# Rows of x by ACT's queue, key weights by SyncE's, and new instruction orders in a four-layer attention kernel

## The chip, the cores and the metric

The kernel runs on one core of a Trainium2 chip. The time is the device time of one execution in microseconds (us); lower is better. Several executions are timed and the median is given. One further execution is recorded by the profiler; its trace is what the profile lines below come from. TensorE (PE) multiplies matrices, VectorE (DVE) and ScalarE (ACT) do elementwise work, GpSimd (POOL) small constants and masks, and SyncE (SP) issues most of the DMAs. Each engine executes its own list of instructions in order and waits on semaphores for the others.

## The reference

The input x has 2048 rows of 512 numbers. Four layers follow one another, of two kinds, and the two weights sets A and B are each used twice:

```python
x = x + A(layernorm(x), A_wqkv, A_wo)   # linear attention, 32 heads of 16
x = x + B(layernorm(x), B_wqkv, B_wo)   # sliding window of 256, softmax
x = x + A(layernorm(x), A_wqkv, A_wo)
x = x + B(layernorm(x), B_wqkv, B_wo)
```

In A, `phi(t) = where(t > 0, t + 1, exp(t)) + 1e-6` is applied to queries and keys, the sums `kv = sum_s phi(k) v` and `z = sum_s phi(k)` run over all 2048 rows, and the output is `phi(q) kv / (phi(q) z + 1e-6)` times `wo`. In B, each row attends to itself and the 255 rows before it.

## The kernel before, in words

The rows are 16 tiles of 128. The work has three parts with two barriers between them, because the sums of a layer A need all rows. Part one (`layer_a_keys`) loads the tiles, normalises them, and computes the keys of the first layer A (`a_k`), their products with the normalised rows (named g) and the queries (`a_q`). After the first barrier, part two (`middle(2)`) runs for each tile the output of layer A, layer B, and the keys of the second layer A. After the second barrier, part three (`middle(3)`) does the same for the last two layers and writes the result.

A tile's normalisation (`norm`) is: statistics on DVE (line 374), their aggregation (line 375), adding epsilon (line 377 on DVE, 379 on POOL), the power -1/2 on POOL (line 380), and subtract and scale on DVE (line 381). The result is transposed: the first five tiles by TensorE (line 395) with a copy by ACT (line 402), the others by a transposing DMA that SyncE issues (line 389). The key product is line 420, the products g line 524, the queries line 480. `phi` is an exponential on ACT (line 444), a minimum on DVE (line 447) and a maximum, either in one DVE instruction (line 451) or with a second ACT instruction (446) and a DVE one (449).

At the first barrier, copies of the sums (named ge, line 407) feed TensorE, a masked product (line 574) and a reciprocal (line 603) follow on DVE, and the weights of the output are merged on TensorE (line 578). In the layers B, ACT computes the exponentials of the scores (lines 720, 755, 788, 835), DVE or POOL the masks (728, 807; 806), and a copy of the keys (bke, line 661 on ACT, 662 on DVE) is spread by DMA.

The loads are issued ahead of everything else: `setup` lists them for SyncE. `xs(a, b)` loads the rows of tiles a to b-1 and names the load after a, so that x0 and x1 are one tile each (128 KB), x2, x4 and x6 two tiles, x8 and x12 four. `w(...)` loads 512 KB of weights: wAq, wAv and wAk are the query, value and key columns of A_wqkv, and wBn is 1 MB of B_wqkv. A load given an earlier load in its last argument is issued only once that one has landed. In `run`, `play` writes each engine's program. Before the planned instructions, DVE clears a tile, TensorE runs nine matmuls on it and then `fill` ones that the plan places (line 277); their results are used by nobody. ACT waits for the cleared tile and issues the two halves of the key weights wAk (line 1117), on which the first two key products wait (`ksem`).

The order of all 2,572 planned instructions, the engine of those that can run on two, and the PSUM bank of each of 1,006 tiles are read from a packed table (`TABLE`, read by `place`); it is the outcome of a search that isn't part of the kernel. `synchronise` then derives the waits from the order. On POOL, an instruction of the names in `LONG` also waits for the last DVE instruction of the names in `SHORT` ahead of it.

## Time and profile before

| | us |
|---|---|
| median of 3 runs | 407.45 |
| lowest and highest | 407.4, 408.07 |
| the profiled execution | 409.25 |
| its span, first to last instruction | 407.4 |
| mean granted TensorE clock | 0.998 |
| busy in the span: TensorE | 386.1 |
| ACT | 350.4 |
| DVE | 349.3 |
| POOL | 125.8 |

A line of a profile view gives start and length in microseconds, then the engine, the line of the kernel, the operation, and the tile it writes, an arrow, and the tiles it reads. `xres` holds the rows of x, `vp` the normalised rows and the keys, `XQ` the transposed rows and the queries, `wA` the weights of layer A, `ps` a bank of PSUM. Square brackets give the idle time ahead of an instruction and what ended it. SPq and ACTq are DMA issues of SyncE and ACT. A busy TensorE is not a TensorE at its peak, since the ends of matmuls are modelled.

### The profile page before, as it was taken

What the parts mean: (1) busy time and instruction counts of PE and PEld (TensorE: products, weight loads), DVE (VectorE), ACT (ScalarE), POOL (GpSimd) and SP (SyncE); (2) the same over time, 40 slices, a digit from 0 to 9 for tenths busy, and PEclk for the clock granted to TensorE, in tenths of its full rate; (3) what the DMA queues carried; (4) which work ended last, traced back from release to release, by engine and by line L of the source; (5) the groups of instructions that cost most, each with busy time, mean ns of one, the idle gap of its engine ahead of it and who ended that gap; (6) DMA issues with size and microseconds to landing.
All of it is one profiled execution on the core that took longest, in us unless ns stands there. A gap on an engine that the chain in (4) does not pass through costs nothing.

```text
span 407.4 us, 17007 instructions
## 1 busy us (share of the span) xinstructions
PE 386.1 (95%) x7394; PEld 255.7 (63%) x7466; DVE 349.3 (86%) x818; ACT 350.4 (86%) x447; POOL 125.8 (31%) x215
## 2 busy tenths in 40 slices
PE   7999999999999999999999999999999989998996
PEld 3644576667475567565656767676656756666674
DVE  5998899999999899888877799998899689777674
ACT  2843559999999999999999368999999999999992
POOL 3588752122243142331602122301203241320130
PEclk9999999999999999999999999999999999999999
DMA  7546324443233425553222100562324433572551
GB/s 253 138 113 163 98 42 107 101 101 81 68 101 78 91 82 121 80 108 80 77 49 56 27 2 2 121 122 69 80 55 101 119 89 68 111 142 77 85 148 40
DMA packets 66986, 37.15 MB, mean 91 GB/s; under 512 B 47648, under 2 KB 62368, under 8 KB 66912
## 3 DMA queue, kind: packets, MB, share of 16 engines
q1 hardware_dynamic: 66080, 34.75, 36.8%
q8 instruction: 59, 0.97, 1.1%
q0 software_dynamic: 288, 0.79, 0.5%
q10 hardware_dynamic: 544, 0.52, 0.4%
q14 instruction: 15, 0.12, 0.1%
HBM read 6.29 MB, written 2.10 MB: 21 GB/s over the span
## 4 chain that ended last, share of the span: by engine, by line
PE 54%; ACT 21%; DVE 14%; issue 5%; DMA 3%; POOL 1%; SPq 1%; POOLq 0%; DVEq 0%
PE ps L420 19%; ACT pb L720 16%; PE ps L856 11%; PE ps L434 8%; PE ps L710 6%; PE ps L480 4%; DVE stats L374 2%; ACT pb L835 2%; PE ps L524 2%; DVE XQ L625 2%; ACT vp L720 2%; DMA xres<-in_A_x_dram 1%; DVE xres L638 1%; DVE vp L451 1%; PE ps L826 1%
## 5 line engine op out<-in xcount | busy, mean ns | idle before, releaser
L720 ACT ACTIVATE pb<-ps 128x1024 bf16<-128x1024 f32 (+2 forms) x216 | 199.4, 1021 | 3.6 <-PE ps L710 2.4
L856 PEld LDWEIGHTS ps<-vB,pb 128*128 128x128 bf16 x2560 | 78.6, 96 | 11.4 <-issue 3.6
L856 PE MATMUL ps<-vB,pb 128*128 128x34 bf16 x2560 | 84.4, 177 | 0.3
L806 POOL TENSOR_SCALAR_AFFINE_SELECT pb<-pb 128x1024 bf16<-128x1024 bf16 x33 | 37.9, 1150 | 106.0 <-DVE pb L807 40.1
L434 PE MATMUL ps<-xT,wBp 128*128 128x128 bf16 x1024 | 69.6, 219 | 0.9 <-ACT pb L720 0.5
L434 PEld LDWEIGHTS ps<-xT,wBp 128*128 128x128 bf16 x1024 | 59.2, 98 | 13.3 <-issue 4.7
L444 ACT ACTIVATE tE<-ps 128x512 bf16<-128x512 f32 x64 | 37.8, 606 | 24.4 <-PE ps L420 9.9
L379 POOL TENSOR_SCALAR ve<-mv 128x1 f32<-128x1 f32 x63 | 16.4, 260 | 130.3 <-DVE mv L375 128.4
L710 PE MATMUL ps<-XQ,kB 32*128 32x256 bf16 (+3 forms) x992 | 48.1, 267 | 3.0 <-DVE o L869 0.5
L420 PE MATMUL ps<-wA,XQ 128*128 128x512 bf16 x175 | 45.3, 379 | 1.7 <-issue 0.5
L638 DVE TENSOR_TENSOR xres<-ps,xres 128x512 bf16<-128x512 f32 x63 | 42.8, 683 | 4.7 <-PE ps L420 4.2
L374 DVE BATCH_NORM_STATS2 stats<-xres 128x6 f32<-128x512 bf16 x64 | 43.2, 681 | 4.0 <-DMA xres<-in_A_x_dram 3.5
L728 DVE TENSOR_TENSOR pb<-pb,tri 128x512 bf16<-128x512 bf16 (+1 forms) x108 | 43.0, 407 | 3.8 <-ACT pb L720 2.9
L380 POOL TENSOR_TENSOR rs<-ve,negh 128x1 f32<-128x1 f32 x64 | 40.3, 630 | 7.6 <-DVE ve L377 2.4
L835 ACT ACTIVATE pb<-ps 128x1024 bf16<-128x1024 f32 x40 | 39.4, 1054 | 1.1 <-PE ps L826 1.1
L480 PE MATMUL ps<-XQ,wA 128*128 128x256 bf16 x256 | 34.1, 273 | 0.4 <-ACT pb L720 0.4
L710 PEld LDWEIGHTS ps<-XQ,kB 32*128 32x128 bf16 x992 | 15.0, 92 | 28.8 <-ACT pb L720 7.6
L420 PE MATMUL ps<-M,XQ 128*128 128x512 bf16 x113 | 30.5, 380 | 2.4 <-issue 0.6
L420 PE MATMUL ps<-wBv,xT 128*128 128x512 bf16 x109 | 30.3, 380 | 2.3 <-issue 1.4
L420 PE MATMUL ps<-wBo,oT 128*128 128x512 bf16 x107 | 28.9, 380 | 2.6 <-DVE tE L447 0.7
L869 DVE TENSOR_TENSOR o<-ps,rc 128x256 bf16<-128x256 f32 x64 | 27.0, 423 | 1.6
L480 PEld LDWEIGHTS ps<-XQ,wA 128*128 128x128 bf16 x256 | 23.6, 98 | 7.5 <-ACT pb L720 0.8
(132 smaller groups left out, 543.8 us busy)
## 6 DMA issues: line engine op xcount, KB each, us to landing
vB<-vS SPq DMA_DIRECT2D x64, 136.0 KB, 2.5
kB<-vp SPq DMA_DIRECT2D x60, 128.0 KB, 2.1
out_dram<-xres SPq DMA_DIRECT2D x9, 128.0 KB, 2.2
wA<-in_A_wqkv_dram SPq DMA_DIRECT2D x2, 512.0 KB, 5.5
xres<-in_A_x_dram SPq DMA_DIRECT2D x2, 512.0 KB, 4.0
pb<-in_B_wqkv_dram SPq DMA_DIRECT2D x1, 1024.0 KB, 6.6
xres<-in_A_x_dram SPq DMA_DIRECT2D x3, 256.0 KB, 5.5
out_dram<-xres POOLq DMA_DIRECT2D x6, 128.0 KB, 2.6
```

Source lines behind the costliest of these rows:

```text
L374: self.on("DVE", "stats", lambda e: e.bn_stats(K.stats[:, t, :], x()), key, dve(512), rd=rd, wr=[("stats", t)], **held)
L380: self.pow = self.on("POOL", "pow", lambda e: e.tensor_tensor(K.rs[:, t, :], K.ve[:, t, :], K.negh[:], ALU.pow), key + 0.03, (640, 690), r ...
L420: m = e.matmul(K.ps(ps), lhs(c), rhs(c), start=c == 0 and not whole, stop=c == 3)
L434: m = e.matmul(K.ps(ps)[:, f * P:(f + 1) * P], w(c, f), xT(c), start=c == 0, stop=c == 3)
L480: m = e.matmul(K.ps(ps)[:, 256 * h:256 * h + 256], K.wA[:, c, f * P:(f + 1) * P], xT(c), start=c == 0, stop=c == 3)
L638: self.on("DVE", "res", lambda e: e.tensor_tensor(K.xres[:, t, :], K.ps(po), K.xres[:, t, :], ALU.add), key, dve(512), rd=[("xres", t)], w ...
L710: m = e.matmul(K.ps(ps[gq])[:, ns * i:ns * i + ns], K.kB[rows, j % 4, 2 * f + b, :, :], K.XQ[rows, f, q:q + ns], start=True, stop=True, ti ...
L720: return e.activation(out(2 * h, 2, ns), i, ACT.Exp, bias=0.0, scale=0.25)
L728: return e.tensor_tensor(x, x, K.tri[:, 0, sh:64].unsqueeze(1).unsqueeze(1).to_broadcast([P, 4, n, 64 - sh]), ALU.mult)
L806: return e.affine_select(out=x, in_=x, compare_op=ALU.is_ge, fill=0.0, base=-2, pattern=[[0, 16], [-2, 64]], channel_multiplier=1)
L835: return e.activation(far(h), i, ACT.Exp, bias=0.0, scale=0.25)
L856: m = e.matmul(K.ps(ps)[:, 34 * u:34 * u + 34], K.P((b // 2) % rp)[:, gq, f, o:o + P], K.vB[:, (b // 2) % 4, b % 2, r, :], start=i == 0, s ...
```

## The change

The loads of tile 1 (x1) and of tiles 2 and 3 (x2) are issued by ACT, ahead of its other work and without a wait. In front of them ACT issues a small read of four pieces of A_wqkv's first columns into an unused row of `kB` (the touch, `tsem`); the first key copy of layer B that SyncE issues (kd) waits for it, because it writes there. The two halves of the key weights become planned loads of SyncE, in its list right behind x0, and every key product waits for its half. The wait of ACT for the cleared tile goes.

All of the table is new. Its entries, decoded, say that SyncE's first issues are x0, wAk0, wAk1, x4, wAq, x6, wAv, x8, a transpose, x12 and wBn; before they were x0, x1, x2, x4, x6, wAq, x12, x8, two transposes and wBn. TensorE's first entries were four fillers, the transpose of tile 0, a filler, the transpose of tile 1, a filler, and the first halves of the keys of tiles 0 and 1; they become two fillers, the transpose of tile 0, four fillers, the transpose of tile 1, and the two halves of tile 0 and then of tile 1. On DVE, tile 1's subtract and scale moves ahead of tile 2's aggregation. On POOL, five constants (c6, c7, c8, c11, c12) move up among the powers of tiles 3 to 8. At the first barrier a copy ge goes from ACT to DVE and a maximum (line 449) from behind it to an earlier place. Further on, 41 instructions change engine: one bke in the first layer B from ACT to DVE, one in the second from DVE to ACT and a copy sc from ACT to DVE, 12 masks of line 806/807 from DVE to POOL and 11 back, five output DMAs from SyncE to POOL and two back, and some copies and memsets. Otherwise neighbours change places, and 364 of the 1,006 tiles have another bank.

```diff
+ACT_LOADS = ("x1", "x2")
...
-        seq += [xs(0, 1), xs(1, 2), w("wAq", "wA", "A_wqkv", 0, 512), xs(2, 4), xs(4, 6), xs(6, 8), xs(8, 12)]
+        def wk(h):
+            return ("wAk%d" % h, lambda e: e.dma_start(K.wA[:, 2 * h:2 * h + 2, 512:1024], K.A_wqkv.rearrange("(k p) c -> p k c", p=P)[:, 2 * h:2 * h + 2, 512:1024]), 262144, [("wAk", h)])
+
+        seq += [xs(0, 1), wk(0), wk(1), xs(1, 2), w("wAq", "wA", "A_wqkv", 0, 512), xs(2, 4), xs(4, 6), xs(6, 8), xs(8, 12)]
...
-            begun.append(self.load(n, f, b, r, key + i if i < 7 else 100.5 + 0.5 * i, begun[i - 4:i - 3] if i >= 6 else []))
+            begun.append(self.load(n, f, b, r, key + i if i < 9 else 100.5 + 0.5 * i, begun[i - 4:i - 3] if i >= 8 else []))
...
-        ps = self.tok("k", t, xT, lambda c: K.wA[:, c, 512:1024], lambda h: [("XQ", t)], key)
+        ps = self.tok("k", t, xT, lambda c: K.wA[:, c, 512:1024], lambda h: [("XQ", t), ("wAk", h)], key)
...
-            ksem, half = [cx.enter_context(nc.semaphore(f"s_key{h}")) for h in range(2)], []
+            tsem, touched = cx.enter_context(nc.semaphore("s_touch")), []
...
                 if name == "ACT":
-                    e.wait_ge(wsem, 1)
-                    for h in range(2):
-                        e.dma_start(self.wA[:, 2 * h:2 * h + 2, 512:1024], self.A_wqkv.rearrange("(k p) c -> p k c", p=P)[:, 2 * h:2 * h + 2, 512:1024]).then_inc(ksem[h], 16)
+
+                    e.dma_start(self.kB[0:1, 3, 0:4, :, :].rearrange("p k n a -> p k (n a)"), self.A_wqkv.rearrange("(k p) c -> p k c", p=P)[0:1, :, 0:128]).then_inc(tsem, 16)
+                    for o in order:
+                        if o.name in ACT_LOADS:
+                            o.emit(e).then_inc(dsem[o.dma[1] % ring], 16)
...
-                    if o.eng != name:
+                    if o.eng != name or o.name in ACT_LOADS:
                         continue
...
-                    if o.name == "k" and len(half) < 2:
-                        e.wait_ge(ksem[len(half)], 16)
-                        half.append(o)
+                    if o.name == "kd" and not touched:
+                        touched.append(1)
+                        e.wait_ge(tsem, 16)
```

## The prediction

> **What bounds the kernel now.** I read the page first, then the windows by stage, then the chain of waits, then the timeline of the first microseconds.

> ```profile
> span 407.4 us, 17007 instructions
> PE 386.1 (95%) x7394; PEld 255.7 (63%) x7466; DVE 349.3 (86%) x818; ACT 350.4 (86%) x447; POOL 125.8 (31%) x215
> ```

> The shares are averages, so the stages decide. In the windows the columns are the stretch, its length, busy time and instructions of PE, weight loads, DVE, ACT and POOL, then the granted clock, the DMA share and GB/s.

> ```profile
> 5.00:10.00 5.00, 4.14 (x24) 1.73 (x23) 3.13 (x9) 1.19 (x2) 1.81 (x6) 1.00 1.02 343
> 10.00:15.00 5.00, 4.95 (x41) 3.47 (x40) 4.93 (x16) 4.22 (x8) 3.56 (x10) 1.00 0.42 123
> ...
> 40.00:45.00 5.00, 4.92 (x64) 2.83 (x67) 3.09 (x6) 2.00 (x4) 4.58 (x8) 1.00 0.77 251
> ...
> 100.00:150.00 50.00, 47.36 (x1013) 30.33 (x1020) 47.43 (x110) 49.15 (x57) 16.03 (x26) 1.00 0.35 86
> 150.00:200.00 50.00, 48.52 (x990) 31.67 (x999) 43.26 (x101) 48.92 (x56) 15.61 (x26) 1.00 0.47 94
> ```

> From 10 us on TensorE has no holes in the first stage (4.95 and 4.92 of 5 us), and DVE is as full as TensorE at 10 to 15. In the attention stage ACT is the full engine (49.15 and 48.92 of 50). So a microsecond saved before 10 us moves the whole first stage, if DVE and TensorE both start sooner; in the attention only ACT's time counts.

> The chain of waits over the start (start, length, engine):

> ```profile
> 1.72 5.19 DMA xres<-in_A_x_dram
> ...
> 6.93 0.71 DVE stats L374
> 7.66 0.18 DVE mv L375
> ...
> 44.50 0.69 DVE kB L407
> 45.19 0.55 DVE XQ L449
> 45.74 0.87 DVE rec L603
> ```

> It begins with a load of rows of x, named x2 in the code (tiles 2 and 3), goes on with DVE, and is on DVE again at the first barrier (44.5 us on: a copy of a sum, a maximum, a reciprocal). The timeline says what the load holds up:

> ```profile
> 6.77 0.40 PE L395 MATMUL ps<-ident,vp 128*128 128x128 bf16 x4
> ...
> 6.93 0.69 DVE L374 BATCH_NORM_STATS2 stats<-xres 128x6 f32<-128x512 bf16 x1 [1.83 <-DMA xres<-in_A_x_dram]
> ...
> 7.76 0.38 DVE L381 TENSOR_SCALAR vp<-xres,mv,rs 128x512 bf16<-128x512 bf16 x1
> ...
> 8.21 0.40 PE L395 MATMUL ps<-ident,vp 128*128 128x128 bf16 x4 [0.81 <-DVE vp L381]
> ...
> 8.44 0.38 PE L277 MATMUL ps<-kB 128*128 128x512 bf16 x1
> ...
> 8.65 1.24 PE L420 MATMUL ps<-wA,XQ 128*128 128x512 bf16 x4
> ...
> 15.95 1.27 DVE L374 BATCH_NORM_STATS2 stats<-xres 128x6 f32<-128x512 bf16 x2
> ```

> DVE executes in order: the statistics of tile 2 wait 1.83 us for x2, and tile 1's normalisation (7.76) stands behind them although tile 1 came long before. TensorE transposes tile 1 at 8.21, runs a filler matmul at 8.44 and starts the first key product at 8.65. Real TensorE work of the stage begins there. At 15.95 come the first statistics of the tiles of x8.

> **The change, part by part.** Decoding the two tables of the diff gives the orders. The same instructions run, apart from the loads.

> *Loads.* SyncE's queue was x0, x1, x2, x4, x6, wAq; it becomes x0, wAk0, wAk1, x4, wAq, x6, wAv, x8. ACT issued the two key-weight halves after waiting for DVE's memset; now it issues a small read of A_wqkv (the touch), x1 and x2 with no wait.

> ```profile
> 0.80 2.37 SPq L294 DMA_DIRECT2D xres<-in_A_x_dram  x5
> ...
> 1.23 0.99 ACTq L1117 DMA_DIRECT2D wA<-in_A_wqkv_dram  x2
> ...
> 7.21 0.60 ACT L402 ACTIVATE XQ<-ps 128x512 bf16<-128x512 bf16 x1 [3.68 <-PE ps L395]
> ```

> The second view below is of the two ACT issues alone, the third a window of one microsecond:

> ```profile
> DMA to landing us min/median/max: 3.9/4.6/5.4
> ...
> 4.00:5.00 1.00, 1.00 (x3) 0.30 (x2) 0.96 (x3) 0.00 (x0) 0.67 (x2) 1.00 0.83 274
> ```

> An issue takes 2.37/5 = 0.47 us on SyncE and 0.50 on ACT. x2 was third on SyncE: issued at 0.80 + 2 x 0.47 = 1.7. As third on ACT, if ACT too begins at 0.8, it is issued at 0.8 + 2 x 0.5 = 1.8. No gain in issue. What lies beside it on the DMA engines is shown by the packets (columns: packets, MB, share) in 0 to 4.25 us, first two lines, and 0 to 5.25 us, last two; q1 is SyncE's queue, q10 ACT's:

> ```profile
> q1 hardware_dynamic: 383, 0.36, 28.5%
> q10 hardware_dynamic: 265, 0.26, 20.2%
> ...
> q1 hardware_dynamic: 500, 0.47, 29.5%
> q10 hardware_dynamic: 427, 0.42, 25.3%
> ```

> In that microsecond q1 gained 0.11 MB and q10 0.16 MB: they share. Before x2 can be complete, x0, x1, wAk0, x2 and most of wAk1 are moved in either order. The best case is that half of wAk1 (0.13 MB) falls behind x2: 0.13 MB / 274 GB/s = 0.48 us sooner. The worst is that ACT's queue starts late, by as much as its whole first issue pair costs on top of the touch, 0.50 + 0.47, less the 0.43 us by which ACT starts earlier (1.23 to 0.80): 0.54 us later. I take 0, the middle. The touch adds an ACT issue of 0.5 us; ACT sat idle for 3.68 us before its first work at 7.21, so it costs nothing, and would cost 0.5 without that idle time. The new wait on the touch stands on SyncE ahead of the first key copy of the sliding layer, with value copies and output DMAs queued behind it; the touch has landed long before. wAq moves up, x6 goes behind it, and x8 behind wAv's 0.5 MB, 1.9 us at that rate. x8 is read only from 15.95 us on, and it no longer follows x12, an equal amount: hidden, and if that cover goes DVE stands up to 1.9 us. x12 and the load of B's weights now come after the first transpose that SyncE issues, with the other transposes behind them; they move up with x8, and I count 0.

> [...]

> *Start of TensorE's work.* The new DVE order puts tile 1's normalisation directly behind tile 2's statistics, ahead of their aggregation: 7.76 - 7.66 = 0.10 us. The new TensorE order has no filler between tile 1's transpose and the key products: 8.65 - 8.44 = 0.21 us. Six fillers instead of five stand ahead of tile 1's transpose (two before tile 0's, four behind it): one more, at most 0.38, which lies in TensorE's 0.81 us of idle there and would cost 0.38 without it. The keys of tile 0 now go as one pair, which needs wAk1 by 8.3 us. It landed at 1.72 + 5.4 = 7.1 as ACT's second issue, and is issued at 0.80 + 2 x 0.47 = 1.7 as SyncE's third: 1.2 us to spare. Term: -0.31 us.

> *First barrier.* The 0.55 us maximum (line 449) leaves the chain ahead of the reciprocal; one copy of a sum (ge) goes from ACT to DVE, ahead of the wait for z, where DVE has room (3.09 of 5 us).

> ```profile
> 47.44 0.84 PE L578 MATMUL ps<-wAo,pqd 128*128 128x512 bf16 x3 [0.35 <-DVE pqd L574]
> ```

> TensorE had other work and stood only 0.35 us here, so at most 0.35 can come back, and at worst the copy (0.69 us on DVE in the chain) comes in its place if it is late: between -0.35 and +0.34. I take -0.30, nearer to the idle time that the row shows.

> *Attention.* One key copy (bke) leaves ACT for DVE:

> ```profile
> L661 ACT ACTIVATE vp<-ps x1: 748/748/748, 156.8 to 156.8; 128x512 bf16<-128x512 f32 x1
> ...
> 154.88 1.89 PE ps L434 x32
> ...
> L806 POOL TENSOR_SCALAR_AFFINE_SELECT pb<-pb x33: 1137/1147/1208, 86.4 to 390.6; 128x1024 bf16<-128x1024 bf16 x33
> ...
> L807 DVE TENSOR_TENSOR pb<-pb,tri x17: 678/682/1103, 87.9 to 381.9; 128x1024 bf16<-128x1024 bf16 x17
> ```

> ACT is full there and DVE has 50 - 43.26 = 6.74 us of room, which says -0.75; but the chain of waits until 156.77 runs on TensorE, which says 0. I take half, -0.37. In the second layer one copy goes from ACT to DVE (sc) and one back (bke): 0. Twelve far masks move from DVE to POOL and eleven back, three output DMAs net from SyncE to POOL, two small memsets change place: nothing on the chain waits for POOL there; without that cover a mask costs DVE 0.68 or POOL 1.15 us. The remaining swaps of neighbours, and other PSUM banks for 364 of 1006 tiles, can close holes or open them; ACT's holes from 100 to 200 us sum to 0.85 + 1.08 = 1.93 us, which bounds both sides. I take 0.

> Sum: -0.10 - 0.21 - 0.30 - 0.37 = -0.98 us. The profiled execution took 409.25 us, of which 407.40 is span; it stands 0.44% above the median of 407.45, and I put the difference on the median: **406.5 us**.

> **The rivals.** *No measurable change, 407.1 us.* The barrier's hole opens elsewhere and bke was hidden; only the 0.31 at the start is kept. For it: DVE is full right after the start (4.93 of 5), so a lead of TensorE may run dry; against it: DVE starts 0.10 sooner too.

> *Slower, 408.5 us.* POOL computes the power that every normalisation waits for. The new order puts five constants among the first nine tiles' powers, which before ran in gaps from 28 us on:

> ```profile
> 32.39 0.21 POOL L328 MEMSET hot<- 128x128 bf16 x1 [0.48 <-DVE tE L447]
> ...
> 32.88 0.36 POOL L337 TENSOR_SCALAR_AFFINE_SELECT hot<-hot 128x128 bf16<-128x128 bf16 x1
> ...
> 28.04 0.12 POOL L328 MEMSET eps<- 128x32 bf16 x1
> ...
> 37.66 0.31 POOL L338 TENSOR_SCALAR_AFFINE_SELECT hot<-hot 128x128 bf16<-128x128 bf16 x1
> ...
> 30.04 0.29 POOL L343 MEMSET eps<- 1x32 bf16 x1
> ...
> L447 DVE TENSOR_SCALAR tE<-tE x64: 229/284/989, 11.9 to 295.3; 128x512 bf16<-128x512 bf16 x64
> ```

> They sum to 1.29 us on a POOL that is 3.56 of 5 busy at 10 to 15, where DVE cannot wait. And DVE's minimum (line 447) has taken up to 0.99 instead of 0.28 us: one such meeting adds 0.7. Together 2.0 us, 406.47 + 2.0 = 408.5. It decides once more than 0.98 + 0.82 = 1.8 us is lost. Against it: POOL has 1.44 us free in that window.
> [...]

> *A larger gain, 405.0 us.* x2 lands 0.48 sooner and half of ACT's 1.93 us of holes close: 406.47 - 0.48 - 0.97. For it: both orders are new throughout; against it: the shared packets.

> **How the numbers follow.** This kernel's runs tell 0.2%, 0.82 us, from no change. Chances: the forecast 0.37, the larger gain 0.13, no change 0.25, slower 0.25. So faster 0.50, same 0.25, slower 0.25. The range goes from the larger gain, 405.0, to a little past the slower rival, 408.7; the forecast's own is 405.9 to 407.0 by the bounds of x2.

> **What would show it.** Right: DVE's wait for x2 still ends near 6.9; the first key product starts near 8.3; TensorE's wait at line 578 is under 0.1; the first stage's last product ends 0.3 sooner; ACT's full stage begins 0.6 sooner. Wrong: normalisations that wait for POOL between 9 and 16 us, a DVE wait for x8 or x6, x2 past 7.4, or new ACT holes between 100 and 200 us.

## The result: slower by 1.3%, and the profile after

The changed kernel takes 413.07 us (median of 4 executions, 411.02 to 413.51) against 407.42 us (407.38 to 408.07) for the kernel before beside it: ratio 1.0125, 95% interval 1.0089 to 1.0161. A second set of executions gave 1.0140 (1.0115 to 1.0166). I had forecast 406.5 us, and a range of 405.0 to 408.7: the sign was wrong and the time lies outside the range. The profiled execution took 413.51 us, 411.8 of it span. In the kernel after, lines stand five further down than before (420 is 425, 374 is 379, 578 is 583).

The head of its page, and the chain of waits over the first 26 us (start, length, what):

```profile
span 411.8 us, 17013 instructions
PE 386.9 (94%) x7395; PEld 255.3 (62%) x7466; DVE 348.6 (85%) x818; ACT 350.9 (85%) x446; POOL 128.5 (31%) x219
```

```profile
0.80 1.21 ACTq L1121
2.44 5.47 DMA xres<-in_A_x_dram
7.93 0.69 DVE stats L379
...
18.29 6.76 DMA XQ<-vp
```

TensorE is as busy as before (386.9 against 386.1 us), so most of the 4.4 us of span are holes. The chain names two of them. It begins no longer with x2 at 1.72 but with the small load (line 1121), whose issue holds ACT's queue for 1.21 us; x2 is on its way from 2.44 and DVE has it at 7.93, before at 6.93. Then a transpose of the first stage takes 6.76 us to land.

The timeline of ACT's queue and of DVE over the same start:

```profile
0.80 1.21 ACTq L1121 DMA_DIRECT2D kB<-in_A_wqkv_dram  x1
2.04 0.85 ACTq L296 DMA_DIRECT2D xres<-in_A_x_dram  x2
```

```profile
2.95 0.69 DVE L379 BATCH_NORM_STATS2 stats<-xres 128x6 f32<-128x512 bf16 x1 [1.75 <-DMA xres<-in_A_x_dram]
...
5.81 0.69 DVE L379 BATCH_NORM_STATS2 stats<-xres 128x6 f32<-128x512 bf16 x1 [1.77 <-DMA xres<-in_A_x_dram]
...
6.64 0.38 DVE L386 TENSOR_SCALAR vp<-xres,mv,rs 128x512 bf16<-128x512 bf16 x1
7.93 0.69 DVE L379 BATCH_NORM_STATS2 stats<-xres 128x6 f32<-128x512 bf16 x1 [0.91 <-DMA xres<-in_A_x_dram]
```

DVE waits three times for rows of x where it waited twice before. The middle wait, 1.77 us, is for x1: it too now stands behind the small load, and tile 0's normalisation (6.64), ready earlier, stands in order behind tile 1's statistics.

The windows from 5 us on (columns as in the prediction), and the waits between 14 and 46 us:

```profile
5.00:10.00 5.00, 3.38 (x19) 1.22 (x17) 3.24 (x8) 1.17 (x2) 1.69 (x5) 1.00 0.93 297
10.00:15.00 5.00, 4.95 (x37) 3.10 (x37) 4.89 (x17) 3.88 (x9) 3.39 (x9) 1.00 0.55 178
...
20.00:25.00 5.00, 4.02 (x22) 2.05 (x21) 5.00 (x16) 3.11 (x6) 3.66 (x8) 1.00 1.18 160
...
100.00:150.00 50.00, 46.89 (x1006) 30.23 (x1012) 46.82 (x110) 48.60 (x58) 12.91 (x22) 1.00 0.39 89
150.00:200.00 50.00, 48.49 (x989) 31.56 (x999) 43.47 (x103) 48.08 (x54) 17.25 (x26) 1.00 0.41 91
```

```profile
PE ps L425 <- DMA XQ<-vp: 1.0, 1, 1.0
```

TensorE loses 0.76 us at 5 to 10 (3.38, before 4.14) and 0.93 at 20 to 25, where it waits 1.0 us for a transposed tile. The kernel before has no such wait between 14 and 46 us, and this row for the same window:

```profile
20.00:25.00 5.00, 4.95 (x43) 2.88 (x42) 4.92 (x14) 3.31 (x6) 4.19 (x9) 1.00 0.67 183
```

ACT's busy time from 100 to 200 us falls (98.07 before, 96.68), but the time does not, so ACT waits more. The transposes' landing from 12 to 46 us, in the view of the tile they fill, first before, then after:

```profile
DMA to landing us min/median/max: 2.4/2.5/5.8
```

```profile
DMA to landing us min/median/max: 2.4/2.5/6.8
```

So one transpose lands late in both kernels: in both it is the one of tile 6, issued right behind the 1 MB load wBn. What is new is that tile 7's transpose, which stood ahead of wBn, now stands behind it too. Before, TensorE took up tile 7 first (23.36 us) and tile 6 at 24.03; after, it takes tile 6 at 25.10 and tile 7 at 27.06.

One more place appears in TensorE's timeline:

```profile
343.29 0.68 PE L784 MATMUL ps<-XQ,kB 32*64 32x32 bf16 x64
345.25 0.81 PE L425 MATMUL ps<-M,XQ 128*128 128x512 bf16 x3 [1.28 <-issue]
```

Behind 64 short matmuls TensorE stands 1.28 us, and no wait for data, engine or bank is named ("issue"). The kernel before stands 0.16 us at this place:

```profile
340.89 0.81 PE L420 MATMUL ps<-M,XQ 128*128 128x512 bf16 x3 [0.16 <-issue]
```

To see where the time goes in each experiment I compare starts: for all instructions that begin within one stretch of 10 us of the first trace of the kernel before, the median difference of start to the same instruction of the other trace. Minus is ahead, in us; the head of a column is the start of the stretch. In the first column of the traces with a new order of the first stage, single instructions also changed places, and these medians are rougher.

| trace | 10 | 40 | 110 | 300 | 340 | 400 |
|---|---|---|---|---|---|---|
| after | 0.54 | 1.41 | 2.34 | 2.54 | 4.37 | 4.25 |
| loads_only | 0.48 | 0.45 | 0.45 | 0.46 | 0.46 | 0.35 |
| orders_only | -0.93 | -0.60 | 0.18 | 0.53 | 1.66 | 1.87 |
| no_touch | -1.43 | -0.49 | 0.01 | 0.18 | 1.37 | 0.64 |
| no_touch_again | -1.37 | -1.00 | -0.10 | 0.31 | 2.30 | 2.12 |
| loads_no_touch | -0.96 | -0.99 | -0.99 | -0.97 | -0.97 | 0.90 |
| touch_last | -1.40 | -1.21 | -1.21 | -1.21 | -1.21 | 0.24 |
| head_new | -1.52 | -1.13 | -1.01 | -0.60 | 0.34 | 0.20 |
| no_touch_shift | -0.96 | -0.66 | -0.18 | 0.08 | 0.14 | -0.49 |
| after_shift | 1.05 | 2.12 | 2.61 | 2.82 | 2.88 | 2.20 |
| tail_new | -1.36 | -1.39 | -1.39 | -0.56 | -0.50 | -0.69 |
| before_stop | -0.29 | 0.78 | 0.79 | 0.81 | 1.64 | 1.54 |
| before_again | -0.42 | -0.06 | -0.06 | -0.06 | -0.06 | -0.04 |

The changed kernel loses at the start, by 40, by 110 and between 300 and 340 us. The experiments take these places one by one.

### The profile page after: what moved, and what is told of

The parts are those of the page before. It is cut to its first block, busy times and chain, and to the rows that moved or that the text cites. A ratio compares the mean times of both kernels' runs of the same rounds, so it can differ in the third digit from the quotient of the medians.

```text
span 411.8 us, 17013 instructions
## 1 busy us (share of the span) xinstructions
PE 386.9 (94%) x7395; PEld 255.3 (62%) x7466; DVE 348.6 (85%) x818; ACT 350.9 (85%) x446; POOL 128.5 (31%) x219
## 4 chain that ended last, share of the span: by engine, by line
PE 45%; ACT 25%; DVE 16%; issue 5%; DMA 4%; POOL 2%; ACTq 0%; POOLq 0%; DVEq 0%
ACT pb L725 20%; PE ps L425 16%; PE ps L861 9%; PE ps L439 7%; PE ps L715 5%; PE ps L485 3%; DVE stats L379 3%; PE ps L529 3%; DVE xres L643 2%; ACT pb L840 2%; DMA XQ<-vp 2%; ACT vp L725 2%; DVE XQ L630 2%; POOL pb L811 1%; DMA xres<-in_A_x_dram 1%
## 5 line engine op out<-in xcount | busy, mean ns | idle before, releaser
L449 ACT ACTIVATE tE<-ps 128x512 bf16<-128x512 f32 x64 | 37.9, 603 | 20.2 <-PE ps L425 6.8
L733 DVE TENSOR_TENSOR pb<-pb,tri 128x512 bf16<-128x512 bf16 (+1 forms) x108 | 42.1, 395 | 2.4 <-ACT pb L725 2.3
L385 POOL TENSOR_TENSOR rs<-ve,negh 128x1 f32<-128x1 f32 x64 | 38.8, 606 | 7.4 <-DVE ve L382 2.3
L425 PEld LDWEIGHTS ps<-wA,XQ 128*128 128x128 bf16 x192 | 16.9, 97 | 18.9 <-DMA XQ<-vp 1.5
```

The source lines that it names most:

```text
L385: self.pow = self.on("POOL", "pow", lambda e: e.tensor_tensor(K.rs[:, t, :], K.ve[:, t, :], K.negh[:], ALU.pow), key + 0.03, (640, 690), r ...
L425: m = e.matmul(K.ps(ps), lhs(c), rhs(c), start=c == 0 and not whole, stop=c == 3)
L733: return e.tensor_tensor(x, x, K.tri[:, 0, sh:64].unsqueeze(1).unsqueeze(1).to_broadcast([P, 4, n, 64 - sh]), ALU.mult)
```

## The experiments

Ratios are to the kernel before, run beside on the same chip, with 95% intervals.

### The two halves of the change

**loads_only**: the loads of the changed kernel (small load, x1, x2 on ACT; key weights second on SyncE), with the order, engines and banks of before.

```
-TABLE = (new order, engines, banks)
+TABLE = (order, engines, banks of before; wAk0 and wAk1 put behind x0)
```

> The new loads (touch, x1 and x2 by ACT, key weights by SyncE right behind x0), with every other instruction in the order, on the engine and in the PSUM bank of the kernel before. Theory 1 (the touch's issue of 1.21 us on ACT pushes x1 and x2 back): x2 lands near 7.9 instead of 6.9 us and the whole kernel is 0.9 to 1.4 us slower than before. Theory 2 (the loads are harmless and the new order costs everything): 407.4, no change.

Measured: 411.11 us (409.6 to 415.18), 1.0108 (1.0047 to 1.0170). The four executions scatter: 409.6, 409.74, 412.49 and 415.18. The profiled one is the quickest, so its trace, only 0.45 us behind, does not show the whole loss; the slowest had a mean granted clock of 0.992, the others 0.999 to 1.000.

**orders_only**: the reverse, the new table on the loads of before.

```
-TABLE = (of before)
+TABLE = (new order, engines, banks, without wAk0 and wAk1)
```

> The new order, engines and banks, with the loads of the kernel before (no touch, rows by SyncE, key weights by ACT). Theory 1: 2.5 to 4 us slower than before, the part of the change that does not come from the start. Theory 2: the full 5.6 us slower. If the order were as good as I predicted, 0.5 to 1 us faster than before.

Measured: 410.70 us (410.36 to 411.13), 1.0066 (1.0051 to 1.0081). Both halves are slower. The new orders are 0.93 us ahead at 10 us, 0.60 at 40, and 1.87 behind at 400.

**after_again**: the changed kernel once more, on the same chip.

> The changed kernel once more, to see how its time scatters. Its four runs lay between 411.02 and 413.51, those of before between 407.38 and 408.07. If the 1.28 us hole of TensorE at 344 us is in the order, it is there again; if it is an accident of one execution, the profile lacks it and the span is shorter by about 1.1 us.

Measured: 413.6 us (412.92 to 414.98), 1.0140 (1.0115 to 1.0166). Its profiled execution shows what the late start can become. Two rows of its chain and two of its windows:

```profile
0.80 1.21 ACTq L1121
...
2.44 6.88 DMA xres<-in_A_x_dram
```

```profile
5.00:10.00 5.00, 2.27 (x11) 0.68 (x9) 1.82 (x5) 0.60 (x1) 0.96 (x3) 0.92 0.78 255
10.00:15.00 5.00, 4.58 (x18) 2.32 (x19) 4.34 (x14) 1.29 (x3) 2.91 (x8) 0.50 0.72 214
```

x2 took 6.88 us instead of 5.47; TensorE was busy 2.27 of 5 us. It stood 0.87 us before its work at 6.88, worked until 8.15 and stood again until 10.42; the granted clock fell to half at 9.18 us and came back at 16.01, 6.8 us later (means of 0.92, 0.50 and 0.90 in the windows that begin at 5, 10 and 15 us), and the schedule is 4.33 us behind in that stretch. When the clock fell TensorE had stood for 1.03 us on end, of 2.27 us in all. In shift_wbn_act below the clock was at half once, for 3.41 us (a mean of 0.66 from 25 to 30 us), where TensorE waited 3.0 us. What sets the fall and how long it lasts, no run shows.

### The small load

**no_touch**: the changed kernel without the small load. Nothing uses its data; only the wait for it goes with it.

```
-                    e.dma_start(self.kB[0:1, 3, 0:4, :, :]..., self.A_wqkv...[0:1, :, 0:128]).then_inc(tsem, 16)
...
-                    if o.name == "kd" and not touched:
-                        touched.append(1)
-                        e.wait_ge(tsem, 16)
```

> The changed kernel without the touch: ACT issues x1 and x2 at once. Theory 1: x1 is issued at 0.8 instead of 2.04 us, x2 lands near 6.7, and the kernel is 1.0 to 1.3 us faster than the changed one, about 411.8. Theory 2: within 0.3 us of the changed kernel, 413.0.

Measured: 411.17 us (409.99 to 411.77), 1.0073 (1.0052 to 1.0094). Its chain begins

```profile
0.80 2.68 DMA xres<-in_A_x_dram
```

and DVE waits for x once, 2.31 us, for tile 0; x1 and x2 are there when it asks. At 10 us it is 1.43 us ahead of before, at 40 us 0.49. The rest of the loss stays.

**loads_no_touch**: loads_only without the small load. **touch_last**: loads_only with the small load issued behind x1 and x2.

```
                     for o in order:
                         if o.name in ACT_LOADS:
                             o.emit(e).then_inc(dsem[o.dma[1] % ring], 16)
+                    e.dma_start(self.kB[0:1, 3, 0:4, :, :]..., self.A_wqkv...[0:1, :, 0:128]).then_inc(tsem, 16)
```

> The new loads (x1 and x2 issued by ACT, key weights second and third on SyncE) without the one-partition load of key weights into kB, with the order, engines and banks of the kernel before. Theory (the small load costs at the start, the loads themselves help): x2 lands near 5.3 us as in the kernel without that load, the first-stage work starts about 1 us sooner than in the kernel before, the lead holds to the end because no later step has changed: 406.4 us (406.0 to 406.9). Rival (the lead is lost again to waits for x6, x8 or the query weights, which now come one place later): 407.2 to 407.8, and DVE shows waits for x6 or x8 before 20 us.

> The new loads with the order, engines and banks of the kernel before, and with the one-partition load of key weights issued by ACT behind x1 and x2 instead of ahead of them. Theory (that load costs because x1 and x2 are issued 1.21 us later): x1 and x2 land as without it (3.7 to 4.1 and 5.2 to 5.8 us), and the time is that of the new loads without it, 408.4 us (407.8 to 409.0). Rival (the transfer itself disturbs the others on the DMA engines, wherever it is issued): x2 lands at 7 us or later, or the executions scatter over more than 4 us, and the time is 410 us or more.

Measured: loads_no_touch 408.37 us (407.82 to 410.95), 0.9998 (0.9972 to 1.0023); touch_last 409.58 us (407.4 to 414.73), 1.0013 (0.9979 to 1.0047). ACT's queue in touch_last:

```profile
0.80 0.91 ACTq L296 DMA_DIRECT2D xres<-in_A_x_dram  x2
1.74 1.16 ACTq L1122 DMA_DIRECT2D kB<-in_A_wqkv_dram  x1
```

The small load costs the same 1.2 us of issue, but neither x1 nor x2 stands behind it, and the start is 1.40 us ahead of before (0.96 without it). By the interval the loss of loads_only is gone or nearly so. The rival's late x2 did not come. Its scatter did, but the kernel before scattered beside it too (407.64 to 412.44 us). Of twelve executions of touch_last the four above 410.8 us had a mean granted clock of 0.992 to 0.996, the other eight (407.4 to 409.79 us) 0.999 or 1.000; why the clock was lower there is in no trace.

**after_touch_last**: the same edit in the whole changed kernel; **no_touch_again**: no_touch beside it.

> The changed kernel whole, with the small load issued by ACT behind x1 and x2 instead of ahead of them. Theory (the small load costs only through the 1.21 us by which it delays the issue of x1 and x2): the time of the changed kernel without it, 410.5 to 411.5 us, x2 landed by 5.8 us. Rival (its transfer costs wherever it is issued): 412.5 us or more.

> The changed kernel without the small load, unchanged from its first run, for its ratio on one chip beside the next three. 1.0073 before. Theory (its loss is the stop of TensorE near 342 us, 1.1, the transposes behind 1 MB between 20 and 40 us, 0.8, and the attention between 80 and 110 us, 0.5, against about 0.9 gained at the start): 1.003 to 1.008, and the stop is there again. Rival (its first four executions were slow by chance): under 1.002.

Measured: 411.27 us, 1.0056 (1.0039 to 1.0073), and 411.37 us, 1.0058 (1.0035 to 1.0080). The two are the same within their intervals: the transfer costs nothing that these runs resolve, its place at the head of the queue does. Against the changed kernel's 1.0125 and 1.0140 that place is worth about 0.7 to 0.8%, some 3 us. Of these, 2.0 us are in the traces at 10 us (0.54 behind with it, 1.43 ahead without); where the rest goes is not located.

I had expected loads_no_touch to beat before, since its trace is 1 us ahead for 350 us. There the lead goes: TensorE's rows at that place in loads_no_touch and in touch_last, and the chain of the first:

```profile
361.99 1.04 PE L425 MATMUL ps<-wBo,oT 128*128 128x512 bf16 x4 [1.63 <-DMA oT<-o]
```

```profile
361.62 1.04 PE L425 MATMUL ps<-wBo,oT 128*128 128x512 bf16 x4 [1.45 <-DMA oT<-o]
```

```profile
357.71 4.24 DMA oT<-o
```

The transpose on SyncE's queue was issued 0.6 us later than in the kernel before although the rest is a microsecond earlier, because a value copy ahead of it took 1.89 us to issue; it then landed in 4.24 us. Before, the copy took 0.60 us and the transpose landed in 3.82; TensorE did not wait. SyncE's rows, first in loads_no_touch, then in the kernel before, then in before_again (the run below):

```profile
355.78 1.89 SPq L694 DMA_DIRECT2D vB<-vS  x1
357.71 1.30 SPq L394 DMA_TRANSPOSE oT<-o  x1
```

```profile
356.50 0.60 SPq L689 DMA_DIRECT2D vB<-vS  x1
357.14 1.85 SPq L389 DMA_TRANSPOSE oT<-o  x1
```

```profile
356.55 1.82 SPq L689 DMA_DIRECT2D vB<-vS  x1
358.42 1.29 SPq L389 DMA_TRANSPOSE oT<-o  x1
```

The slow copy is not the cause by itself: in before_again it took 1.82 us, the transpose was issued later still, and TensorE did not wait, for the landing took 2.50 us. What sets these issue and landing times no run shows, so how the lead goes is seen, and why is open.

**before_again** asks whether the first trace of the kernel before was itself late at the start, since its execution (409.25 us) stands above the medians.

> The kernel before, unchanged, with a second profile. Its first profiled execution took 409.25 us, 1.1 to 1.8 us above its medians, so a difference read against that one trace is too favourable by as much. Theory (what varies between its executions is the landing of the first loads): this profile's execution takes 407.4 to 408.4 us, x2 lands earlier than the 6.91 us of the first profile, and the whole schedule is 0.8 to 1.5 us ahead of the first profile from 10 us on. Rival (what varies are single late transfers or late instructions anywhere): the two traces agree up to 20 us within 0.3 us and part at one later place.

Measured: 408.59 us (407.55 to 409.94), 0.9993 (0.9966 to 1.0020); profiled execution 409.09. My theory fell: the second trace is 0.42 us ahead at 10 us, loses that where TensorE waits 0.3 us for a transposed tile, and agrees within 0.06 us from 40 us on. So even under the order of before a lead at the start is not kept. What the quicker, unprofiled executions have less is in no trace. A lead of under a microsecond in a trace is not yet a lead in the median.

### Where the new order loses

**head_new**: no small load; new order up to position 606 (about 75 us), the order of before from there.

```
+TABLE = (new[0:606] + before[606:], banks carried over the seam)
```

> No small load; the new order, engines and banks up to position 606 of the list (about 75 us), the ones of the kernel before from there on. Theory (the new order loses in three separate places: by 40 us 0.8, at 80 to 110 us 0.6, near 342 us 1.1): only the first loss is left, the time is 406.8 us (406.3 to 407.4), ACT's wait for TensorE at 80 to 110 us is that of the kernel before, and the stop of TensorE near 341 us is under 0.4 us. Rival (the losses after 75 us come from what the new first stage leaves behind): about 408 us or more, with the same waits at 80 to 110 us as in the changed kernel.

Measured: 410.11 us (408.57 to 411.9), 1.0025 (0.9999 to 1.0052): above the forecast. In its trace the loss at 80 to 110 us is not there: ACT's wait in that stretch, first in head_new, then in the changed kernel:

```profile
ACT pb L725 <- PE ps L715: 0.9, 3, 0.4
```

```profile
ACT pb L725 <- PE ps L715: 1.8, 5, 0.6
```

The kernel before has 0.9 too:

```profile
ACT pb L720 <- PE ps L710: 0.9, 3, 0.4
```

Over all the traces the split is complete: 0.9 us in the eight with the order of before in this stretch (before, before_again, before_stop, loads_only, loads_no_touch, touch_last, tail_new, head_new), 1.8 in the ten with the new one. The windows of no_touch from 100 us on:

```profile
100.00:150.00 50.00, 46.91 (x999) 30.07 (x1005) 46.39 (x111) 49.26 (x58) 13.95 (x25) 1.00 0.37 83
150.00:200.00 50.00, 48.48 (x992) 31.64 (x1000) 43.33 (x100) 48.06 (x55) 18.29 (x26) 1.00 0.46 96
```

So it is the new order of the attention itself that makes ACT, the full engine there, wait twice as long. The loss by 40 us is in the head: of 1.52 us of lead at 10 us 1.13 are left.

**no_touch_wbn**: in no_touch, the 1 MB load wBn is moved on SyncE from behind the first transpose to behind the fourth.

```
-SyncE: T5, x12, wBn, T6, T7, T8, T10, ...
+SyncE: T5, x12, T6, T7, T8, wBn, T10, ...
```

> The changed kernel without the small load, and with the 1 MB load wBn issued behind the transpose of the ninth tile on SyncE instead of behind that of the sixth. Theory (the transposes of tiles 6 to 8 land late since 1 MB is moved ahead of them, and TensorE waits for XQ): TensorE's wait for XQ between 15 and 27 us falls from about 2.6 us (matmul and weight load together) to under 1 us, and the lead over the kernel before at 40 us grows by 0.4 to 0.8 us; the time is 0.4 to 0.8 us under the kernel without the small load. Rival (that wait is covered by ACT's or DVE's work, which sets the first stage): the wait falls and the time at 40 us stays; or wBn's own matmuls at 44 us wait for it.

Measured: 411.81 us (410.4 to 414.0), 1.0078 (1.0051 to 1.0106), no better. The hole moved along with the load and grew. Windows of no_touch, then of no_touch_wbn with its waits:

```profile
20.00:25.00 5.00, 3.89 (x23) 1.91 (x21) 4.39 (x12) 2.57 (x4) 3.14 (x8) 1.00 0.84 84
25.00:30.00 5.00, 5.00 (x25) 2.28 (x24) 4.87 (x16) 1.19 (x2) 3.18 (x7) 1.00 0.38 80
```

```profile
20.00:25.00 5.00, 5.00 (x29) 2.58 (x28) 4.96 (x14) 2.67 (x5) 3.63 (x9) 1.00 0.43 81
25.00:30.00 5.00, 3.28 (x16) 1.35 (x15) 5.00 (x17) 1.19 (x2) 3.56 (x8) 1.00 1.12 286
```

```profile
PE ps L425 <- DMA XQ<-vp: 1.7, 1, 1.7
```

The transposes behind 1 MB are late, whichever they are (the latest takes 6.8 us to land in no_touch and 5.9 in no_touch_wbn, the median 2.5 in both); the rival that something else sets the first stage is not borne out, for TensorE's busy time falls where the load stands.

**shift_wbn_act**: no_touch_shift (below) with wBn issued by ACT.

```
+                    if o.name == "wBn":
+                        if name != "ACT":
+                            continue
+                    elif o.eng != name or o.name in ACT_LOADS:
-                    if o.eng != name or o.name in ACT_LOADS:
```

> The changed kernel without the small load, with the twelve waits on TensorE, and with the 1 MB load wBn issued by ACT, so on another queue than SyncE's transposes. Theory (TensorE's wait for XQ between 20 and 25 us is the transposes of tiles 6 and 7 standing behind that 1 MB on SyncE's queue): those transposes land within 3 us of their issue, the wait falls under 0.4 us, and the time is 0.5 to 0.9 us under the kernel with the twelve waits, 408.3 us. Rival (the DMA engines are busy with the 1 MB whichever queue it comes from, or ACT's own issue and its wait for x8 cost as much): the transposes still take over 4 us, and the time stays at 409.0 us or more.

Measured: 409.38 us (408.42 to 413.08), 1.0012 (0.9986 to 1.0039); no_touch_shift has 1.0009. Nothing gained. In the profiled execution, its slowest, a transpose is on its way for 8.75 us and TensorE waits 3.0:

```profile
16.76 8.75 DMA XQ<-vp
```

```profile
PE ps L425 <- DMA XQ<-vp: 3.0, 1, 3.0
```

The rival fits: this transpose was issued on SyncE 0.58 us ahead of wBn, which ACT issued at 17.34 us, and was late all the same, so it did not stand behind wBn in a queue. What stood ahead of it on SyncE, x12, had landed by 17.61 us; wBn landed at 25.16 and the transpose at 25.51, so the two, issued by different engines, were under way together for 7.82 us (17.34 to 25.16). It is one trace, its moment of issue is not the same as on SyncE, and an earlier issue by ACT stays untried.

### The stop near 342 us

It is in all seven traces that hold the new order of the last 100 us and TensorE's instructions at their places in its stream (0.60 to 1.34 us).

**no_touch_shift** and **after_shift**: twelve waits on a semaphore that has long been set, on TensorE behind its warm-up (the nine matmuls ahead of the planned instructions). In the compiled program they are six instructions, so TensorE's later instructions stand six places further along, and nothing else differs.

```
                     for _ in range(9):
                         e.matmul(self.PS[:, SPARE, :], warm[:, 0:P], warm, start=True, stop=True)
+                    for _ in range(12):
+                        e.wait_ge(wsem, 1)
```

> The changed kernel without the small load, and with twelve more waits on a semaphore that has long been set, put on TensorE behind its warm-up matmuls, so that each later TensorE instruction moves by about twelve places in its instruction stream. Theory (the 1.3 us stop of TensorE near 342 us is a late block of instructions, and its place is set by where the blocks end): the stop falls below 0.5 us or moves elsewhere, and if it is gone the time is about 1.0 us under the kernel without the small load. Rival (the stop is a wait for data, a bank or an engine): it stays at 1.2 to 1.5 us at the same matmul.

> The changed kernel whole, with twelve waits on a long-set semaphore behind TensorE's warm-up matmuls, which move its later instructions by six places. Theory (the stop near 342 us depends on where the instruction stream is cut): no stop over 0.5 us there, and 411.5 to 412.6 us, about 1.1 us under the changed kernel. Rival (the stop comes from the new order's waits): the stop stays at 1.0 to 1.5 us and the time at 413.0 us or more.

Measured: no_touch_shift 409.05 us (408.25 to 411.47), 1.0009 (0.9983 to 1.0035), where no_touch has 1.0073 and 1.0058; after_shift 411.84 us (411.17 to 412.15), 1.0067 (1.0042 to 1.0093), where the changed kernel has 1.0125 and 1.0140. The place in after_shift:

```profile
342.93 0.68 PE L784 MATMUL ps<-XQ,kB 32*64 32x32 bf16 x64
343.77 0.81 PE L425 MATMUL ps<-M,XQ 128*128 128x512 bf16 x3 [0.16 <-issue]
```

The stop is gone in both, and in shift_wbn_act, which holds the twelve waits too. It is no wait for data, since order, waits, banks and loads are the same. By the ratios the shift is worth 0.5 to 0.7%, some 2 to 3 us, more than the one stop; the intervals are about 1 us wide to each side, and what else it spares the unprofiled executions no trace shows.

Where are such stops? The page of a profile lists a queue of instruction packets (packets, MB, share), after; before it shows the same 59 and 0.97:

```profile
q8 instruction: 59, 0.97, 1.0%
```

In the trace each of the 59 packets has 16384 bytes. TensorE's compiled stream has 15170 instructions of 64 bytes in the kernel after, 0.97 MB like the packets; if these are its own, a packet holds 256 instructions. The weight loads are complete in all 18 traces, so trace and compiled stream can be matched one to one. After the first 30 us, ten stops of over 0.35 us stand at an instruction that has nothing to wait for, in nine traces; all ten are at place 196 or 197 when places are counted modulo 256. The seven stops near 342 us stand at place 196 as well. I call these places, 256 apart, cuts. Three of the ten, from head_new, no_touch_wbn and before_stop:

```profile
340.87 0.20 PE L784 MATMUL ps<-XQ,kB 32*64 32x32 bf16 x1 [0.74 <-issue]
```

```profile
321.30 0.61 PE L784 MATMUL ps<-XQ,kB 32*64 32x32 bf16 x56 [0.41 <-issue]
```

```profile
320.93 0.60 PE L779 MATMUL ps<-XQ,kB 32*64 32x32 bf16 x55 [0.67 <-issue]
```

They stop in the middle of 64 matmuls of one shape: before the last one, behind the eighth, behind the ninth, wherever the cut falls. In the changed kernel the cut near 342 us stands directly behind the 64, with the twelve waits three matmuls before their end. That the short matmuls run through a packet's instructions fast (64 pairs of weight load and matmul in 0.68 us) may be why the stops stand among them; no run tests it. The places are as far apart as a packet has instructions; that the stops, 0.4 to 1.3 us, have to do with the step from one packet to the next is my estimate from that. What TensorE waits for there no trace shows: in the kernel after a packet is on its way from 342.39 to 343.71 us and the next from 346.15, and none during the stop (343.97 to 345.25).

**before_stop**: the kernel before, with 131 short warm-up matmuls for nine long ones, so that its cut too stands directly behind the 64 near 341 us (TensorE gets 122 more pairs ahead of it).

```
-                    for _ in range(9):
-                        e.matmul(self.PS[:, SPARE, :], warm[:, 0:P], warm, start=True, stop=True)
+                    for _ in range(131):
+                        e.matmul(self.PS[:, SPARE, 0:32], warm[:, 0:P], warm[:, 0:32], start=True, stop=True)
```

> The kernel before with 131 warm-up matmuls of 32 columns in place of nine of 512, so that its later TensorE instructions stand at the same place in their blocks of 256 as in the changed kernel (the last of the 64 short matmuls before the stop: 195 in place of 207). Order, engines, banks and loads are untouched. Theory (late instruction block): a stop of 0.7 to 1.5 us appears behind the 64 short matmuls near 341 us, where the kernel before has 0.16 us, and the time rises to 409.3 to 409.9 us. Rival (the stop belongs to the new order): no stop, 408.2 to 408.8 us.

Measured: 409.48 us (408.21 to 412.12), 1.0018 (0.9996 to 1.0039). At 342 us there is no stop (0.16 us); one of 0.67 us came at the cut near 321 us instead, where the kernel before has none. So the cut says where a stop can be, and not whether it comes: that part of my theory failed, and what makes a stop come stays open. Its 1.0018 is not the price of the stop alone: the trace also loses 1.1 us by 40 us (from 0.29 ahead to 0.78 behind), where TensorE waits 1.0 us for a transposed tile, under the order of before.

**tail_new**: no small load; the order of before up to position 1818 (about 290 us), the new one from there, with the cut again three matmuls before the end of the 64.

```
+TABLE = (before[0:1818] + new[1818:], banks carried over the seam)
```

> No small load; the order, engines and banks of the kernel before up to position 1818 of the list (about 290 us), the new ones from there on. Theory (the new order of the last 100 us gains about 0.6 us once TensorE's stop near 342 us is not there, and in this kernel the instructions stand as far along in their stream as in the kernel without the stop): no stop over 0.5 us near 341 us, and 0.4 to 0.7 us under the new loads without the small load, so 407.8 us (407.3 to 408.3). Rival (the gain of the last 100 us in the trace was time won back after the stop): 408.4 us, the same as without the new tail; or, if the stop belongs to the new order, 409.5 us.

Measured: 408.39 us (407.39 to 409.55), 0.9979 (0.9952 to 1.0006). No stop near 341 us. It has the lowest ratio here, about 0.9 us under the kernel before, and its interval still holds 1 and the 0.9998 of loads_no_touch. It also lost 0.8 us between 170 and 190 us to late transposes, where loads_no_touch, the same program up to there, lost nothing.

## Why the prediction was wrong, step by step

Two steps carry most of the miss by the ratios: the place of the small load (1.0125 and 1.0140 with it in front, 1.0056 to 1.0073 without or behind) and the place of TensorE's instructions in its stream (1.0067 with only this moved). With both mended, no_touch_shift stands at 1.0009, level with before. What the attention and the first stage's transposes lose is there about made up by the earlier start.

- **x2's landing, taken as 0, bounds -0.48 to +0.54.** This step failed: DVE's wait ended 1.0 us later (7.93 for 6.93), 2.4 us later in after_again. The mechanism, order of issue, was right; its size came from the sentence "An issue takes 2.37/5 = 0.47 us on SyncE and 0.50 on ACT." The row behind the 0.50 was of two loads of 256 KB; the small load takes 1.21 us. The upper bound was built from the same 0.50, and the wait ended beyond it. My sign of failure "x2 past 7.4" is what came.
- **"The touch adds an ACT issue of 0.5 us", priced at nothing.** I named as cover ACT's idle time before its first work. ACT's arithmetic was covered; the two loads behind it on the same queue were not, x1 among them, which I did not follow at all. By the ratios this is a loss of about 3 us, next to which the place of TensorE's instructions, 2 to 3 us, cannot be ranked: the intervals are about 1 us wide to each side.
- **Start of TensorE's work, -0.31.** Right in sign and near in size: with the loads of before the new order is 0.93 us ahead at 10 us, of which 0.48 is an earlier x2 in that trace (6.45 for 6.93), and no_touch is 0.47 further ahead than loads_no_touch (1.43 and 0.96). In the changed kernel it is buried: 0.54 behind.
- **x12 and wBn behind the first transpose, "I count 0".** Failed. I looked at what the moved loads themselves are needed for, not at the transposes behind them. A transpose behind wBn takes 6.76 us to land, where the median is 2.5. That lateness is not new (5.8 us before); a second transpose behind the same load is. TensorE's wait is 0.5 to 1.4 us in eight of the nine traces with the new order of the first stage and wBn in its new place on SyncE, and none in after_again. The order of before is not free of it either: 0.3 us in before_again, 1.0 in before_stop.
- **First barrier, -0.30.** TensorE's wait there fell from 0.35 to 0.24 us: a third of it. The bounds held.
- **Attention, -0.37.** Failed. In no_touch, which is level with before in time there, ACT's busy time from 100 to 200 us is 49.26 + 48.06 = 97.32 us, the copy's 0.75 less; but ACT waits longer for TensorE, and between 40 and 110 us between 0.5 and 0.9 us are lost in the six traces of the table that have the new order there. I priced the moved copy and not the order around it.
- **Remaining swaps and banks, 0 within 1.93.** The bound was ACT's holes between 100 and 200 us. The stop near 342 us is on TensorE and no hole of that row bounds it. No term of mine held the place of an instruction in its stream, which by no_touch_shift and after_shift is worth 0.5 to 0.7%.
- **The slower rival, POOL's constants.** It did not come: POOL is busy 3.39 of 5 us at 10 to 15 (3.56 before), and no normalisation waits for POOL between 9 and 16 us. The time rose for other reasons. The 0.7 us was a meeting of DVE's minimum with POOL: in before, the six of its 64 minima that take over 0.30 us run beside memsets, copies and selects on POOL (the 0.99 us from 39.21 beside a memset of 1.03 us from 39.02). In after none of those before 30 us takes over 0.30; so the constants that moved up slowed none there. The larger gain did not come either.
- **The execution above its median.** I scaled the sum to the median. A second trace of the kernel before shows the same schedule, so the difference could not be read from the trace.

## What to carry to other kernels

Before a load is put at the head of a queue, price its issue from a load of its own shape and then count everything that stands behind it on that queue, not only the engine's next arithmetic. A large load moved ahead of small transfers has to be priced by what those wait for. When a trace shows a stop with no releaser behind a run of short matmuls, shift the instruction stream by a few places before looking for a cause in the order: two runs that differ by six instructions tell whether the place matters. They do not tell why it does.
